# Causal attention feeding two feed-forward layers on one core: where the transposes of the probabilities stand in the traced order

## The chip, the cores and the metric

One core of one Trainium2 chip. The metric is the device time of one execution in microseconds: 579.84 us is the median of three runs of the kernel before (579.39 to 580.96).

## What is computed

```
attention: q, k, v of shape (2, 12, 448, 64); per head
    scores = q @ k.T / 8;  causal mask;  p = exp(scores - rowmax);  p = p / (sum(p) + 1e-9)
    out = p @ v                                  -> x of shape (896, 768)
layer 1:  h = relu(x @ w_in); y = (h * h) @ w_out          (768 -> 2048 -> 768)
layer 2:  8 experts; each token goes to the expert with the largest cosine logit,
          out = gate * (relu(y @ w1[e]) @ w2[e])           (768 -> 1024 -> 768)
```

The routing must choose the same expert as an fp32 computation, so the kernel computes in split precision: an operand is kept as a rounded high part and a low part (the rest), and a product is three matmuls, high by high, high by low, low by high.

## The kernel before

**Tiling of the attention.** A unit is one batch and one pair of heads, so there are 12 units. The 448 queries of a head are cut into seven blocks of 64, and one matmul works on the same block of both heads (2 x 64 = 128 rows). Block c needs (c + 1) x 64 keys.

**What is done for a unit.**
- `s_load` (line 162) loads q and k in one DMA and v in another. `s_prep` (line 174) splits them: ScalarE (ACT) writes the high part of q into the tile `qs`, VectorE (DVE) the low part, and two DMAs on SyncE's queue (SP) copy `qs` into `q2` (line 196), where the two heads stand in separate halves. There are two buffers of `qs` and two of `q2`. GpSimd (POOL) makes the low part of k, and the low part of v in `s_prep_v` (line 199).
- `s_scores` (line 210) takes a block: three matmuls into one bank of PSUM (tile `s`, four banks, line 221), then a masked maximum on DVE (line 231), then the exponential on ACT (line 233), which writes `p` to SBUF and frees the bank.
- `s_norm` (line 236) divides: a reciprocal on DVE (line 241), and for each block a multiplication on POOL (line 245). It comes in two groups, the blocks 2, 0, 1, 3 and the blocks 6, 4, 5.
- `s_trans` (line 255) takes one of the four entries of `BANKS` (line 250): four transposes of 128 x 128 on TensorE (PE) fill one bank of PSUM (tile `pt`, three banks in turn), ACT copies the bank to SBUF as the high part (600 ns or so) and DVE subtracts that from the bank as the low part, which frees the bank. Batch 0 needs the blocks 0 to 3, batch 1 the blocks 4 to 6, batches 2 and 3 blocks of both groups.
- `s_pv` (line 268) multiplies by v in four parts j = 0 to 3 (24 matmuls in all). Part 0 reads the transposes of batches 0 and 1, parts 1 and 2 those of batches 2 and 3, part 3 those of batch 1, with 64 rows instead of 128. `s_x` (line 286) then takes the result out of PSUM with ACT and DVE.

**The order.** The loop near the end of the attention walks through half-steps. For every half-step a string says in which order the pieces are traced: `p` is `s_prep`, `s0` to `s2` are up to three groups of score blocks, `n` is `s_norm`, `t0` to `t3` are the four batches of `s_trans`, `v0` to `v3` the four parts of `s_pv`, `w` is `s_prep_v`. In the even half-step of unit u the scores are the blocks 6 (`s0`) and 4, 5 (`s1`) of unit u + 1, the norm is that of the blocks 2, 0, 1, 3 of unit u + 1, the transposes are of unit u and the parts of `s_pv` of unit u - 1. In the odd half-step the scores are the blocks 2, 0, 1 (`s0`) and 3 (`s1`) of unit u + 2 and the norm that of the blocks 6, 4, 5 of unit u + 1.

The traced order is a priority and not yet the order of execution. A planner walks through a simulated timeline, and on each engine takes the earliest traced instruction whose inputs and buffers the timeline has ready; matmuls of a later piece can so stand between two transposes of one batch. The result is a fixed order for each engine, and on the chip each engine runs its own in that order, waiting on semaphores.

**After the attention.** The matmuls of layer 1 (`phase_a`, lines 303 to 305) are traced behind it, and the planner puts the first of them between the transposes and `s_pv` matmuls of the last two units.

```
        for x in CFG["seq"][h].split():
            i = int(x[1])
            ...
            if x[0] == "t" and 0 <= u < NU:
                s_trans(units[u], i)
            if x[0] == "v" and u >= 1:
                s_pv(units[u - 1], i)
```

Of the kernel before, what the change touches and what calls it, by code (L numbers as in the profile page):

```python
# [32 lines left out]
def f32(ap):  # L33
# [6 lines left out]
    turn2=[1, 3], ft0=[0, 1, 2, 3, 4], ft1=[3], ft2=[2, 4, 5, 6], ew=[2, 4, 10, 10, 10, 12, 14], stop=0, mlo="V", xh="A", h2="A",  # L40
    wh="G", wil="G", wol="GV", warm=6, nsa=6, nwi=3, nwb=3, wo0=4, hs0=[4, 5, 8, 9], conv0=17, convs=2, pin=1,
    qsb=2, pb=2, ptb=2, qkraw=3, vraw=2, vb=2, ss=4, pts=3, pvs=1, pas=4, wsp=1, mz="G",
    seq=("p0 s0 n0 t0 v0 s1 v1 s2 t1", "n0 t2 s0 v2 v3 t3 s1 s2 w0"),
    ch=(((2, 0, 1), (3,), ()), ((6,), (4, 5), ())), wn=[1], qh="A", qdir=1, qss=2, rpin=5, qdma="SS", kh="V",
    vh="AG", kl="G", vl="G", pth="AAAA", nrm="GGGGGGG", u0=1, order=[2, 1, 3, 0, 4], pm=1)

# [1148 lines left out]
```

## Time and profile before

| | |
|---|---|
| median of 3 runs | 579.84 us |
| the profiled execution | 578.43 us, of it 576.7 us between the first and the last instruction |
| PE busy | 552.8 us (96%), 3424 matmuls |
| DVE busy | 397.5 us (69%) |
| ACT busy | 290.8 us (50%) |
| POOL busy | 197.1 us (34%) |
| chain of waits that ended last | 82% on PE |
| attention scores on PE (line 221, high part of k) | 168 matmuls, mean 347 ns from issue to end |
| transposes on PE (line 262) | 192, mean 278 ns from issue to end |
| copies of transposes on ACT | 48, mean 600 ns |
| subtractions of transposes on DVE | 48, mean 682 ns |

A matmul's own duration overlaps with the next one's, so the time that it costs is read from the distance between starts, or from the chain of waits, which counts each stretch once.

### The profile page before, as it was taken

To read this page: it belongs to the slowest core of one execution; us is meant where nothing else is said; L and a number is where in the kernel's file an instruction comes from. 1 tells how busy PE (TensorE), PEld (TensorE's weight loads), DVE (VectorE), ACT (ScalarE), POOL (GpSimd) and SP (SyncE) were. 2 spreads that over 40 slices of the span, in tenths; PEclk is the share of its full clock that TensorE was granted. 3 is DMA by queue.
4 is the path that set the end of the run, shared out by engine and by line. 5 is a ranking of instruction groups with operands and counts; after the bars stand their busy time and mean duration, and the time that the engine had idled before them with its cause. 6 is when DMAs were issued, how large, how long until landed. Compare 5 with 4: busy or idle time off the path is not lost.

```text
span 576.7 us, 9694 instructions
## 1 busy us (share of the span) xinstructions
PE 552.8 (96%) x3424; PEld 509.6 (88%) x3424; DVE 397.5 (69%) x956; ACT 290.8 (50%) x654; POOL 197.1 (34%) x228
## 2 busy tenths in 40 slices
PE   7999999999999999999999999899998999999994
PEld 4999899989999999999899999799997887799993
DVE  7888878855687967796663466973487976932641
ACT  4878777424425243415233217611468877914651
POOL 7677788936535543311000001002204701500010
PEclk8799999999999999999999999999999999899998
DMA  7658433332536445351000019205777987940310
GB/s 230 174 144 269 102 86 77 116 110 98 165 116 212 164 165 178 128 190 55 1 29 27 28 45 409 95 2 197 283 260 251 341 301 258 342 155 29 111 51 5
DMA packets 28234, 86.52 MB, mean 150 GB/s; under 512 B 2822, under 2 KB 13062, under 8 KB 28176
## 3 DMA queue, kind: packets, MB, share of 16 engines
q1 hardware_dynamic: 26640, 79.51, 42.4%
q0 software_dynamic: 1536, 6.29, 3.0%
q8 instruction: 29, 0.48, 0.3%
q14 instruction: 29, 0.24, 0.1%
HBM read 75.24 MB, written 6.29 MB: 141 GB/s over the span
## 4 chain that ended last, share of the span: by engine, by line
PE 82%; DVE 6%; ACT 4%; DMA 3%; issue 2%; SPq 0%; POOL 0%; POOLq 0%; ACTq 0%; DVEq 0%
PE yps L515 19%; PE ops L812 8%; PE pa L303 7%; PE pa L305 7%; PE pa L304 7%; PE pv L279 7%; PE s L221 5%; DVE ml L66 3%; PE pt L262 3%; PE hps L722 3%; PE hps L738 2%; PE hps L737 2%; PE hps L739 2%; PE ops L754 2%; PE ops L749 2%
## 5 line engine op out<-in xcount | busy, mean ns | idle before, releaser
L66 DVE TENSOR_TENSOR ml<-xraw,mh 128x768 fp32r<-128x768 f32 x64 | 60.1, 954 | 15.0 <-ACT mh L59 14.9
L59 ACT ACTIVATE mh<-xraw 128x768 fp32r<-128x768 f32 x64 | 53.3, 845 | 18.3 <-PE ops L749 8.5
L221 PE MATMUL s<-kh,q 128*128 128x128 f32 (+6 forms) x168 | 52.0, 347 | 3.0 <-ACT p L233 2.6
L812 PE MATMUL ops<-mh,act 128*128 128x384 f32 x224 | 53.5, 341 | 0.0
L834 POOL DMA_INDIRECT out<-osb,fsi x10 | 23.6, 2358 | 86.3 <-ACT osb L829 63.9
L279 PE MATMUL pv<-pt,v 128*128 128x448 f32 (+7 forms) x288 | 49.9, 304 | 0.0
L245 POOL TENSOR_SCALAR p<-p,rs 128x192 f32<-128x192 f32 (+6 forms) x84 | 42.5, 525 | 11.2 <-DVE rs L241 10.8
L846 POOL DMA_INDIRECT xr<-ydram,fgi x10 | 14.9, 1490 | 88.3 <-DVE fsi L624 47.0
L123 DVE SCALAR_TENSOR_TENSOR w<-raw,w 128x768 int32<-128x768 int32 x32 | 43.1, 1350 | 0.7
L279 PEld LDWEIGHTS pv<-pt,v 128*128 128x128 f32 (+3 forms) x288 | 37.6, 162 | 5.9 <-DVE pt L66 0.3
L233 ACT ACTIVATE p<-s,mn 128x192 f32<-128x192 f32 (+6 forms) x84 | 39.5, 477 | 6.0 <-DVE mn L231 2.6
L66 DVE TENSOR_TENSOR ml<-mraw,mh 128x768 fp32r<-128x768 f32 x32 | 30.1, 953 | 14.4 <-ACT mh L59 14.4
L812 PEld LDWEIGHTS ops<-mh,act 128*128 128x128 f32 x224 | 39.3, 188 | 0.8
L221 PEld LDWEIGHTS s<-kh,q 128*128 128x128 f32 x168 | 34.4, 214 | 6.2 <-ACT p L233 4.7
L66 DVE TENSOR_TENSOR hs<-h,hs 128x512 fp32r<-128x512 f32 (+1 forms) x32 | 21.9, 691 | 23.9 <-ACT hs L59 23.7
L119 DVE TENSOR_SCALAR w<-raw 128x768 int32<-128x768 int32 x32 | 24.2, 755 | 20.3 <-POOL wi3l L66 7.3
L66 DVE TENSOR_TENSOR pt<-pt 128x512 fp32r<-128x512 f32 x48 | 32.5, 682 | 6.9 <-ACT pt L59 6.3
L121 DVE SCALAR_TENSOR_TENSOR w<-raw,w 128x768 int32<-128x768 int32 x32 | 34.5, 1080 | 0.7
L309 ACT ACTIVATE relu<-pa 128x448 f32<-128x448 f32 x32 | 17.1, 538 | 35.3 <-PE pa L305 35.1
L231 DVE CUSTOM_DVE_ANT_0 s<-s,maskf 128x192 f32<-128x192 f32 (+6 forms) x77 | 31.8, 430 | 3.7 <-PE s L221 3.2
L59 ACT ACTIVATE pt<-pt 128x512 fp32r<-128x512 f32 x48 | 28.0, 600 | 10.5 <-PE pt L262 10.3
L262 PE MATMUL pt<-ident,p 128*128 128x128 f32 x192 | 31.7, 278 | 0.0
(462 smaller groups left out, 1646.3 us busy)
## 6 DMA issues: line engine op xcount, KB each, us to landing
xraw<-in_wm SPq DMA_DIRECT2D x32, 768.0 KB, 5.7
raw<-in_w_in SPq DMA_DIRECT2D x16, 768.0 KB, 4.2
raw<-in_w_out SPq DMA_DIRECT2D x16, 768.0 KB, 4.2
mraw<-in_wm SPq DMA_DIRECT2D x16, 768.0 KB, 5.9
qk<-in_qkd SPq DMA_DIRECT2D x11, 448.0 KB, 4.3
q<-qs SPq DMA_DIRECT2D x22, 224.0 KB, 3.8
v<-in_vd SPq DMA_DIRECT2D x12, 256.0 KB, 3.8
ydram<-ysb SPq DMA_DIRECT2D x7, 384.0 KB, 2.3
```

Source lines behind the costliest of these rows:

```text
L59: A.activation(out, in_, AF.Copy, scale=scale)
L66: eng.tensor_tensor(out=lo, in0=x, in1=hi, op=ALU.subtract)
L123: V.scalar_tensor_tensor(out=w[:, x], in0=raw[:, x, 0], scalar=29, in1=w[:, x], op0=ALU.logical_shift_right, op1=ALU.bitwise_or)
L221: T.matmul(ss, d["q2"][:, c, :, :, x].rearrange("p a b -> p (a b)"), d[y][:, :n], start=i == 0, stop=i == 2 and not first)
L245: G.tensor_scalar(out=p, in0=p, scalar1=rs[:, COL[c]:COL[c] + 1], scalar2=1.0, op0=ALU.mult, op1=ALU.mult)
L262: T.transpose(pt[:, o * P:(o + 1) * P], d["p"][c][:, j * P:(j + 1) * P], ident)
L279: T.matmul(d["pv"][:, j * P:S] if h else d["pv"][0:D, j * P:S], d[x][0:k, j, 1:3].rearrange("p a b -> p (a b)") if h else d[x][0:k, j, 0], ...
L303: T.matmul(ps, wh[:, c], xhi[:, kc, gs], start=(kc == 0), stop=False)
L304: T.matmul(ps, wh[:, c], xlo[:, kc, gs], start=False, stop=False)
L305: T.matmul(ps, wl[:, c], xhi[:, kc, gs], start=False, stop=(kc == KC - 1))
L515: T.matmul(ps[t][c][:, :384], x, w[:, c * 384:(c + 1) * 384], start=(f == 0 and w is wh and x is hi), stop=(f == NF - 1 and x is lo))
L812: T.matmul(ps[c], x, ww[:, c * 384:(c + 1) * 384], start=(fc == 0 and x is hh and ww is wh), stop=(fc == 7 and x is hl))
```

## The change

The two strings of the order are replaced. In the even half-step batch 1 moves from the last place to the one behind batch 0; in the odd half-step batch 3 moves from behind `v3` to the place behind batch 2. Nothing else differs: the same instructions, tiles, buffers and engines.

```diff
-    seq=("p0 s0 n0 t0 v0 s1 v1 s2 t1", "n0 t2 s0 v2 v3 t3 s1 s2 w0"),
+    seq=("p0 s0 n0 t0 t1 v0 s1 v1 s2", "n0 t2 t3 s0 v2 v3 s1 s2 w0"),
```

## Rows read from the trace of the kernel before

**Rows 1.** The page's first part: busy time, share of the span, instructions
```profile
PE 552.8 (96%) x3424; PEld 509.6 (88%) x3424; DVE 397.5 (69%) x956; ACT 290.8 (50%) x654; POOL 197.1 (34%) x228
```

**Rows 2.** Stretches of time, with each engine's busy time in it
```profile
core 0: us, PE busy (x) PEld busy (x) DVE busy (x) ACT busy (x) POOL busy (x), PEclk, DMA share, GB/s
16.00:20.40 4.40, 4.40 (x19) 4.23 (x20) 3.18 (x14) 2.82 (x12) 2.88 (x5) 0.51 0.98 246
30.00:104.00 74.00, 73.36 (x529) 66.65 (x529) 61.31 (x201) 57.97 (x177) 58.83 (x104) 1.00 0.52 139
104.00:126.00 22.00, 22.00 (x140) 19.42 (x139) 16.02 (x28) 7.17 (x16) 14.86 (x15) 1.00 0.26 77
126.00:230.00 104.00, 104.00 (x515) 96.21 (x514) 77.21 (x70) 39.29 (x70) 48.72 (x30) 1.00 0.49 160
```

**Rows 3.** Who waited for whom, 20 to 104 us: total us, times, longest
```profile
PE s L221 <- ACT p L233: 0.5, 1, 0.5
...
PEld s L221 <- ACT p L233: 2.4, 7, 0.7
...
ACT qs L59 <- DMA q<-qs: 8.7, 6, 2.3
```

**Rows 4.** The chain of waits, 62 to 84 us: start, us, what
```profile
68.57 0.81 PE s L221 x3
...
73.06 0.33 PE s L221 x3
...
80.72 0.44 PE pt L262 x4
...
82.26 0.51 PE s L221 x3
...
83.33 0.59 PE pt L262 x4
```

**Rows 5.** PE in order of time, 118 to 122 us: start, us, instructions
```profile
118.75 1.03 PE L262 MATMUL pt<-ident,p 128*128 128x128 f32 x8
...
119.83 0.60 PE L262 MATMUL pt<-ident,p 128*128 128x128 f32 x4
```

**Rows 6.** All engines in order of time, 62 to 70 us
```profile
61.95 0.68 DVE L66 TENSOR_TENSOR pt<-pt 128x512 fp32r<-128x512 f32 x1
...
62.82 0.60 PE L262 MATMUL pt<-ident,p 128*128 128x128 f32 x4
...
65.24 0.61 ACT L59 ACTIVATE qs<-qk 128x448 fp32r<-128x448 f32 x1 [2.29 <-DMA q<-qs]
65.26 0.66 PE L262 MATMUL pt<-ident,p 128*128 128x128 f32 x4
...
68.06 0.37 ACT L233 ACTIVATE p<-s,mn 128x128 f32<-128x128 f32 x1
...
68.40 0.60 ACT L59 ACTIVATE pt<-pt 128x512 fp32r<-128x512 f32 x1
...
68.57 0.45 PE L221 MATMUL s<-kh,q 128*128 128x384 f32 x1 [0.47 <-ACT p L233]
```

**Rows 7.** All engines in order of time, 82 to 91 us
```profile
84.04 1.70 POOL L245 TENSOR_SCALAR p<-p,rs 128x448 f32<-128x448 f32 x3 [0.31 <-DVE rs L241]
...
86.16 0.27 PE L262 MATMUL pt<-ident,p 128*128 128x128 f32 x1
86.19 1.76 PE L279 MATMUL pv<-pt,v 128*128 128x448 f32 x8
...
88.11 0.49 PE L262 MATMUL pt<-ident,p 128*128 128x128 f32 x3
```

**Rows 8.** All engines in order of time, 16 to 24 us
```profile
17.73 0.63 PE L262 MATMUL pt<-ident,p 128*128 128x128 f32 x2
...
18.33 1.70 POOL L245 TENSOR_SCALAR p<-p,rs 128x448 f32<-128x448 f32 x3 [1.16 <-DVE rs L241]
...
21.14 0.60 PE L262 MATMUL pt<-ident,p 128*128 128x128 f32 x4
```

## The prediction

> **What bounds the kernel now.** I read the busy times first, then stretches, waits, and the chain. The busy times show PE at 96% of the span and the next engine, DVE, at 69% [rows 1]. Cut into stretches, the attention's steady part from 30 to 104 us has PE busy for 73.36 of 74.00 us at full clock, and DVE, ACT and POOL for 61.31, 57.97 and 58.83 us [rows 2]. So PE sets the pace there, with the three others at 78 to 83%, close enough that a queue in the wrong order can hold PE up. From 104 to 230 us PE is busy in every microsecond [rows 2], with the matmuls of layer 1 filling all that the last two units leave. What is won or lost on PE before 104 us is therefore passed on whole to the end.
>
> The waits show how much there is to win. Between 20 and 104 us PE stood still once, for 0.5 us, and its weight loads seven times for 2.4 us, all for the same thing: the exponential of a score block that had not yet freed its PSUM bank [rows 3]. The reason is one line further down: ACT stood 8.7 us in six waits, the longest 2.3 us, with a high part of q at the head of its queue, until the DMA that still read the `qs` buffer was done; the exponentials queue behind it [rows 3]. One such place is seen in order of time: ACT waits 2.29 us and starts on `qs` at 65.24, the exponential of block 1 comes at 68.06, and at 68.57 PE, idle for 0.47 us, starts block 5 [rows 6].
>
> **The change part by part.**
>
> *The transposes themselves.* Their number stays at 192 in 48 batches. On the chain a batch of four costs 0.44 us, 0.11 us each [rows 4]. The trace already has eight in a row, near the end: their row lasts 1.03 us where the row of four lasts 0.60 [rows 5], so the second four add 0.43, again 0.11 each. Batches of eight are no cheaper and no dearer: 0.00 us, with 0.01 per pair of batches, 24 x 0.01 = 0.24 us, as the bound on the good side and nothing on the bad.
>
> By the Trainium skill ("TensorE: Matmul & The Clock Gate", Part 4: PE-mode transpose) transposes do not count as PE being busy for the clock gate, which speaks against packing them. Here the stretch that holds the eight and the four has its clock granted in full, 1.00 [rows 2], against the rule for a pack of this size. What the rule would cost is the last rival below.
>
> *Behind `v3`.* Batch 3 now runs behind the 64-row matmuls of `v3`, and costs 0.59 us on the chain instead of 0.44 [rows 4]. In the new order a score block stands there. A score block behind 64-row matmuls costs 0.51 us where the same block elsewhere costs 0.33 [rows 4]. The 0.15 that the transposes save the scores pay with 0.18. I take 0; the bounds are -0.15 x 9 = -1.4 us (nine of the twelve units lie in the steady part) and +0.03 x 9 = +0.3.
>
> *Batch 1 ahead of `v0` and of the blocks 4 and 5.* It cannot move far: it needs the blocks 4 to 6 normed. In the unit that I followed POOL norms them from 84.04 to 85.74, the batch's first transpose is at 86.16 and the other three at 88.11, behind eight matmuls with v [rows 7]. So the three can move up by at most about 2 us, into the matmuls with v, and the PE work is merely permuted. Where they get in front of block 5, this block ends 0.44 us later, and what hangs on it is the DMA that refills `q2` (it waits for block 5 of two units before), then ACT's wait for the `qs` buffer, then the exponentials. Behind the waiting `qs` on ACT stand exponentials and copies, behind these DVE's subtractions, and PE waits for all of them. Bounds: 0, where PE has other work, as in all but one of the places of rows 3; 0.44 x 6 = 2.6 us, if each of the six waits of ACT is carried through. I take it once, at the one place where PE itself already stands idle: +0.44 us.
>
> *Batch 3 ahead of the blocks 2, 0, 1 and of `v2`, `v3`.* It moves up from 65.26 to about 63.26, right behind batch 2 (62.82 + 0.44) [rows 6]. It needs the PSUM bank of batch 0, three banks back, whose subtraction ends at 61.95 + 0.68 = 62.63 [rows 6]: free, with 0.63 us to spare. Its copy on ACT, now at 68.40 behind the exponential of block 1 [rows 6], can then stand ahead of the exponentials of 2, 0 and 1, and these each end one copy, 0.60 us, later. But the three exponentials wait in the same queue behind `qs` either way. If the copy goes ahead of `qs`, it is done in ACT's idle time and the backlog behind is 0.60 us shorter; if behind, 0.60 us longer. Bounds -0.60 and +0.60 at each of the six places, -3.6 and +3.6 us, cut on the good side to the 2.4 us of weight-load waits that exist. I take 0, since nothing in the rows says which of the two the planner picks. The DVE subtraction moves with the copy. No DMA is issued by a step that moves; SP's and POOL's queues hold the same instructions, and in the odd half-step the norm still stands first.
>
> *The start.* Up to the first transposes nothing changes. The clock is at half there (0.51 from 16.00 to 20.40 [rows 2]). Batch 1 of the first unit can't come before POOL is done with its blocks at 18.33 + 1.70 = 20.03, and it stands at 21.14 [rows 8]: at most 1.1 us, in a part of PE's queue that is full anyway. 0 us.
>
> *The end of the attention.* In the last two units the transposes stand between matmuls of layer 1 and PE has no gap at all [rows 2]: 0 us.
>
> **Sum.** 0 + 0 + 0.44 + 0 + 0 + 0 = +0.4 us on a span of 576.7. The profiled execution took 578.43 us with what lies around the span, so 578.8; the median of three runs lies 1.4 above the profiled one, so 580.2 us. A difference under 0.3% of the time, 1.7 us, can't be told from none.
>
> **The rivals.**
>
> *A, slower: ACT's waits grow.* The place is the `qs` at the head of ACT's queue. Batch 1 ahead of block 5 delays the refill of `q2` by 0.44 us per unit, the copy of batch 3 falls behind `qs`, and in the six units with an ACT wait PE waits 0.44 us more: 6 x 0.44 = 2.6, 582.4 us. With the copy's 0.60 on top at three of the six, 4.4 us, 584.2. For it: DVE and ACT have little slack, and the wait chain already reaches PE. Against: in six of seven cases PE had enough queued that it lost under half a microsecond. It decides from 1.7 us on, four of six places carried through.
>
> *B, slower: the PSUM banks.* Batch 3 right behind batch 2 finds the bank of batch 0 still being read. The spare time is 0.63 us at the place that I followed [rows 6]. If DVE is later by more than this and PE then waits 0.25 us in each of nine units, 2.3 us: 582.1. Against: a subtraction that the planner sees as late lets it put other matmuls first.
>
> *C, faster: the waits go.* Batch 3's copy runs in ACT's idle time, the 2.4 us of weight-load waits shrink to a fifth or so, and the 0.15 us behind `v3` is saved in three units: 1.9 + 0.45 = 2.4, 577.4 us. For it: the idle time of 2.29 us is there and the copy needs 0.60. Against: the planner must put it ahead of `qs` by its own timeline, in which this DMA need not be late.
>
> *D, nothing moves.* The norms on POOL end just before batch 1 starts, and the planner lets other matmuls pass whatever waits. Then PE's order is nearly the same and the time is 579.8, within the forecast's bound.
>
> *E, the clock.* Were the half clock of the start to last to the end of the fourth batch at 23.7 us because more transposes stand there, the 3.3 us from 20.4 on would yield half their work: +1.6 us, 581.4. The page named above would have it so; the full clock beside the eight transposes speaks against it, and so does the fact that batch 1 hardly moves there.
>
> **How the numbers follow.** Forecast 0.35, A 0.25, B 0.08, C 0.20, D 0.10, E 0.02. Forecast and D together give 0.45 for no difference; A, B and E 0.35 for slower; C 0.20 for faster. The likeliest stands at 580.2. The range reaches down to C's 577.4 with 0.2 of spread, 577.2, and up to A's upper case, 584.2: below and above lie about one in ten each, mostly A carried through in more units.
>
> **What would show it.** In the changed kernel's trace: rows of eight transposes of about 1.03 us between 30 and 104 us, or fours parted by other matmuls, if D holds. PE busy within 0.5 us of 73.4 in a 74 us stretch; scores behind `v3` at about 0.51 us. The waits of `s` for `p` tell A from C: above 4 us for A, under 1 us for C. B shows as transposes that wait for DVE's subtraction, which the trace of before does not have. E shows in the granted clock from 20 to 24 us. The prediction is wrong if the attention ends more than 1.7 us earlier or later, or if the stretches behind 126 us, which I take as shifted and otherwise the same, change their length.

## The result and the profile after

The changed kernel took 584.22 us in the median of its runs (580.20 to 588.14), the kernel before 580.72 in the runs beside them (577.37 to 583.38). The ratio is 1.0064, with a 95% interval of [1.0047, 1.0081]: slower by 0.64%, which is 3.7 us (the two medians are 3.5 apart), and more than the 0.3% that can be told from no change. The forecast of 580.2 was wrong, and the median stands just beyond the upper end of the range, 584.2. The profiled execution took 583.35 us with a span of 581.5 us, 4.8 us more than before.

Busy times of the changed kernel, answering to [rows 1]: PE's share stays at 96%, and this view tells nothing.

```profile
PE 556.2 (96%) x3424; PEld 511.7 (88%) x3424; DVE 396.8 (68%) x956; ACT 290.3 (50%) x654; POOL 197.3 (34%) x228
```

The stretches of [rows 2] in the changed kernel, with 20.4 to 24 and 60 to 90 us added; the columns are those of [rows 2].

```profile
16.00:20.40 4.40, 4.40 (x21) 4.19 (x21) 3.63 (x13) 2.51 (x11) 2.59 (x5) 0.60 0.91 244
20.40:24.00 3.60, 3.55 (x26) 2.96 (x26) 3.41 (x17) 3.60 (x15) 2.40 (x5) 1.00 0.76 146
30.00:104.00 74.00, 71.00 (x487) 63.12 (x488) 55.31 (x183) 51.24 (x162) 51.61 (x93) 0.98 0.48 126
60.00:90.00 30.00, 27.49 (x178) 23.85 (x177) 19.61 (x68) 19.11 (x60) 19.45 (x36) 0.94 0.37 89
104.00:126.00 22.00, 21.90 (x143) 19.63 (x142) 15.90 (x32) 10.29 (x27) 21.05 (x25) 1.00 0.35 109
126.00:230.00 104.00, 104.00 (x521) 95.83 (x520) 79.27 (x77) 38.07 (x69) 48.47 (x30) 1.00 0.46 149
```

The kernel before from 60 to 90 us:

```profile
60.00:90.00 30.00, 29.48 (x213) 26.57 (x211) 23.78 (x82) 23.40 (x73) 22.87 (x40) 1.00 0.45 104
```

PE lost 2.36 us of busy time in the steady part (73.36 to 71.00), 1.99 of them from 60 to 90 us, where it ran 178 matmuls in place of 213. The three other engines did less there too, 3.4 to 4.3 us each: nobody became the bound, they all stood still. Busy time understates the loss, since part of it ran at half clock, as the last section tells: from 30 to 104 us PE ran 487 matmuls in place of 529, and at the pace of before (74.00 us for 529) the 42 that are missing are worth 5.9 us, an estimate. The loss reaches layer 1 whole. Its last weight tile, before and after (x12: shortest, median, longest in ns, first and last start in us), comes 5.6 us later:

```profile
L303 PE MATMUL pa<-xhi,wi15h x12: 362/365/369, 226.3 to 233.0; 128*128 128x448 f32 x12
```

```profile
L303 PE MATMUL pa<-xhi,wi15h x12: 362/365/369, 231.9 to 238.6; 128*128 128x448 f32 x12
```

At the end of the profiled execution 4.8 us of it are left, and 3.5 between the medians; where the rest is made up is not shown.

The waits of the changed kernel, 20 to 104 us, answering to [rows 3] (total us, times, longest):

```profile
ACT qs L59 <- DMA q<-qs: 12.4, 7, 3.9
...
PEld s L221 <- ACT p L233: 4.9, 10, 1.0
ACT p L233 <- PE pt L262: 3.8, 2, 2.0
...
PE s L221 <- ACT p L233: 2.1, 5, 0.8
...
PE pt L262 <- DVE pt L66: 0.4, 1, 0.4
```

ACT's wait in front of `qs` grew from 8.7 to 12.4 us, its longest from 2.3 to 3.9, and PE's waits for the exponentials from 0.5 and 2.4 to 2.1 and 4.9. The place of the longest one, all engines in order of time (start, us, instructions, in brackets the idle time before), answers to [rows 6]:

```profile
61.40 3.22 PE L279 MATMUL pv<-pt,v 128*128 128x448 f32 x20
...
62.34 0.60 ACT L233 ACTIVATE p<-s,mn 128x384 f32<-128x384 f32 x1
...
64.55 1.53 PE L262 MATMUL pt<-ident,p 128*128 128x128 f32 x12
...
66.94 0.62 ACT L59 ACTIVATE qs<-qk 128x448 fp32r<-128x448 f32 x1 [3.92 <-DMA q<-qs]
...
67.44 0.41 ACT L233 ACTIVATE p<-s,mn 128x192 f32<-128x192 f32 x1
...
67.83 1.57 ACT L59 ACTIVATE pt<-pt 128x512 fp32r<-128x512 f32 x3
...
68.00 0.48 PE L221 MATMUL s<-kh,q 128*128 128x448 f32 x1 [0.25 <-ACT p L233]
...
69.30 0.63 PE L262 MATMUL pt<-ident,p 128*128 128x128 f32 x4 [0.42 <-DVE pt L66]
...
70.21 0.35 ACT L233 ACTIVATE p<-s,mn 128x64 f32<-128x64 f32 x1
...
70.71 0.64 PE L221 MATMUL s<-kh,q 128*128 128x320 f32 x1 [0.78 <-ACT p L233]
```

Twenty matmuls with v and then twelve transposes run in a row while ACT waits for the DMA. At 66.94 ACT is let go with `qs`, an exponential and three copies of transposes in its queue, and the exponential of block 0 comes at 70.21. PE has nothing left to do meanwhile but wait for the banks, at 68.00, 69.30 and 70.71. ACT's wait of 3.92 us is 1.6 longer than the 2.29 of before [rows 6], and ACT comes to it at the same time, 63.0 us. The DMA that ends it was issued 0.4 us later (at 61.21 against 60.79) and took 1.2 us longer until ACT was released (5.7 us against 4.5); why it took longer is not shown.

The chain of waits shows what follows one unit later (start, us, what). In before's chain [rows 4] no DMA stands between 62 and 84 us; here one does.

```profile
72.73 0.97 PE s L221 x3
...
75.07 4.25 DMA q<-qs
...
79.48 0.61 ACT qs L59
```

The unit's last score block is late, the two DMAs that refill its `q2` are issued only behind it (the second one at 75.07), and the next `qs` waits for them until 79.48. Behind v3 [rows 4] and in the places of [rows 7, 8] nothing adds up to this: rows of eight hardly occur between 30 and 104 us (fours and twelves do), and near the end, where before had a row of eight [rows 5], there are twelve:

```profile
124.34 1.47 PE L262 MATMUL pt<-ident,p 128*128 128x128 f32 x12
```

PE's order in the program shows why. Each letter is a run of matmuls: s scores, t transposes, v matmuls with v. Two units of the steady part, first before, then after:

```
t4 s6 t3 s3 t1 s3 t1 v8 s3 t3 v4 t4 s3 v1 s3 v11 t4 s6 t4 s6 t4 v8 s3 v4 t4 v2 s3 v3 s3 v7
t4 s3 t4 s3 t4 s3 v16 s3 v2 t4 s3 v6 s6 t3 s3 t1 s6 v21 t12 s6 v3 s6
```

With batch 3 early, a unit's matmuls with v are all ready early. By `BANKS` it reads the blocks 4 to 6 alone, and not blocks of both groups, so it waits for no norm that batch 1 has not waited for. Batch 1 of the next unit still waits for its norms on POOL, so the planner lets some twenty of them pass it, and batches 1, 2 and 3 then come out together, in three units of the steady part.

### The profile page after: what moved, and what is told of

Read it like the earlier page. It is cut to its first block, busy times and chain, and to the rows that moved or that the text cites. A ratio compares the mean times of both kernels' runs of the same rounds, so it can differ in the third digit from the quotient of the medians.

```text
span 581.5 us, 9698 instructions
## 1 busy us (share of the span) xinstructions
PE 556.2 (96%) x3424; PEld 511.7 (88%) x3424; DVE 396.8 (68%) x956; ACT 290.3 (50%) x654; POOL 197.3 (34%) x228
## 4 chain that ended last, share of the span: by engine, by line
PE 78%; DVE 8%; ACT 4%; issue 3%; POOL 3%; DMA 2%; SPq 1%; POOLq 0%; ACTq 0%; DVEq 0%
PE yps L515 19%; PE ops L812 10%; PE pa L305 7%; PE pa L303 7%; PE pa L304 7%; PE pv L279 4%; DVE ml L66 4%; PE s L221 4%; PE hps L722 3%; PE pt L262 2%; PE hps L738 2%; PE hps L737 2%; PE hps L739 2%; POOL p L245 2%; PE ops L754 2%
## 5 line engine op out<-in xcount | busy, mean ns | idle before, releaser
L221 PE MATMUL s<-kh,q 128*128 128x128 f32 (+6 forms) x168 | 53.5, 357 | 3.9 <-ACT p L233 3.7
L279 PE MATMUL pv<-pt,v 128*128 128x448 f32 (+7 forms) x288 | 46.1, 300 | 0.0
```

The lines of the kernel that those rows point to most:

```text
L221: T.matmul(ss, d["q2"][:, c, :, :, x].rearrange("p a b -> p (a b)"), d[y][:, :n], start=i == 0, stop=i == 2 and not first)
L279: T.matmul(d["pv"][:, j * P:S] if h else d["pv"][0:D, j * P:S], d[x][0:k, j, 1:3].rearrange("p a b -> p (a b)") if h else d[x][0:k, j, 0], ...
```

## The experiments

**Theory A**: the loss is ACT's wait in front of `qs`; the new order makes it reach PE and feeds it back through `q2`. **Theory B**: it is the lumpy order itself, which starves ACT and DVE and then floods them. Ratios are against the kernel before, run beside each.

**Which half of the change.** e8 moves batch 3 alone, e7 moves it half the way:

```diff
-    seq=("p0 s0 n0 t0 v0 s1 v1 s2 t1", "n0 t2 s0 v2 v3 t3 s1 s2 w0"),
+    seq=("p0 s0 n0 t0 v0 s1 v1 s2 t1", "n0 t2 t3 s0 v2 v3 s1 s2 w0"),   # e8
+    seq=("p0 s0 n0 t0 v0 s1 v1 s2 t1", "n0 t2 s0 t3 v2 v3 s1 s2 w0"),   # e7
```

> Only the odd half-step's string replaced, the even one as before. The planner gives each engine the same instructions in the same order as in the changed kernel, so every theory expects its time: slower than the kernel before by 0.4 to 0.9%, 582.5 to 586 us. It shows whether the loss is there again beside the other kernels of this call.

> The kernel before with batch 3 moved only half of the way, behind the scores of the blocks 2, 0, 1 and still ahead of the matmuls with v. The planner then puts batches 0 and 1 in a row of eight ahead of 15 to 18 matmuls with v, and has no row of twelve before 104 us. Theory B: no lump of 20 and 12, so within 1.7 us of the kernel before. Theory A: ACT's waits for the DMA decide; above 11 us the time is 583 us or more, under 9 us it is that of the kernel before. If long runs of matmuls with v alone cost (16 to 18 are here too), 582 us or more.

e8: 584.95 us, 1.0078 [1.0050, 1.0106]. Its instructions stand in the changed kernel's order on every engine; with the even string alone replaced, they stand in the order of before on every engine, so that half needed no run. The whole effect is batch 3's. Its profile has no half clock between 30 and 104 us, and layer 1's last tile comes 4.3 us later than before, against 5.6 in the changed kernel; the 1.3 us between them fit the half clock told of at the end.

```profile
L303 PE MATMUL pa<-xhi,wi15h x12: 362/365/369, 230.7 to 237.3; 128*128 128x448 f32 x12
```

e7: 581.77 us, 1.0029 [1.0004, 1.0053], a loss at the edge of what can be told from none. There eight transposes stand in a row in the steady part, twelve never. ACT waits 6.7 us for `qs`, less than in the kernel before, and yet PE's waits for the exponentials, 2.4 and 4.5 us, are those of the changed kernel: neither sum alone sets the loss.

**Eight in a row.** e4 puts both batches of a pair last. Batches 2 and 3 then read blocks of p that a later unit has partly overwritten, so that part of the computation is changed; the work is the same.

```diff
+    seq=("p0 s0 n0 v0 s1 v1 s2 t0 t1", "n0 s0 v2 v3 t2 t3 s1 s2 w0"),
```

> The changed kernel with both pairs of batches moved to the end of their half-step's matmuls with v (batches 0 and 1 last in the even half-step, 2 and 3 behind v3 in the odd one), so that eight transposes do stand in a row but behind the scores. Theory A: the scores of block 5 come earlier, so do the refill of q and ACT's split; ACT's waits for the DMA under 8.7 us, 577 to 581 us. Theory B: rows of eight transposes give ACT and DVE two copies in a lump but no run of 20 matmuls ahead of them; 579 to 583 us. If eight in a row is what costs, whatever stands ahead of it: 583 us or more.

581.31 us, 1.0009 [0.9986, 1.0033], with rows of eight in each unit of the steady part, at 1.03 to 1.09 us, the price of [rows 5]:

```profile
49.85 1.03 PE L262 MATMUL pt<-ident,p 128*128 128x128 f32 x8
...
58.05 1.03 PE L262 MATMUL pt<-ident,p 128*128 128x128 f32 x8
```

Rows of eight cost nothing here; what costs is where batch 3 stands.

**Room for qs, planned anew.** e1 is the changed kernel, e2 the one before, with four of the eleven `qs` tiles (units 2, 3, 6, 7) in buffers that lie free during the attention:

```diff
+    qraw=[2, 3, 6, 7]
-            q = apool.tile([P, NQ, QC, 2], F32R, tag="qs", bufs=CFG["qss"], name="qs")
+            if units.index(u) in CFG["qraw"]:
+                q = spool.tile([P, NQ, QC, 2], F32R, tag="raw", name="qs")
+            else:
+                q = apool.tile([P, NQ, QC, 2], F32R, tag="qs", bufs=CFG["qss"], name="qs")
```

> The changed kernel with two more buffers for the split q (units 2, 3, 6 and 7 take a staging buffer that is idle then), so that ACT seldom finds the buffer still read by a DMA. Theory A (the exponentials queue on ACT behind the split of q, which waits for that DMA; 12.4 us of such waits in the changed kernel against 8.7 before): the waits fall under 4 us between 20 and 104 us, PE's weight loads wait for exponentials under 2.5 us, and the time comes back to the kernel before or below, 577 to 582 us. Theory B (the planner's new order is itself lumpy: some 20 matmuls with v in one run, then 12 transposes, so that ACT and DVE first starve and then have three copies ahead of the exponentials): ACT's waits for the DMA fall as well, but the lumps and most of the loss stay, 582.5 to 586 us.

> The kernel before with the same two extra buffers, as the control. Theory A: ACT's waits for the DMA (8.7 us) fall under 3 us and PE's 2.4 us of waits for exponentials under 1 us; the time falls by 1 to 2 us against the kernel before. Theory B: no lumps here, so nothing to win but the same 1 to 2 us at most. If the extra buffers alone cost or win more than 3 us, the first kernel of this call is to be read against this one and not against the kernel before.

e1: 580.96 us, 0.9998 [0.9979, 1.0017]; the loss is gone. e2: 580.96, 0.9990 [0.9971, 1.0010], without the 1 to 2 us that were expected of it. In e1 the steady part is full, PE busy for 73.88 of 74.00 us. Layer 1's last tile still starts 2.5 us later than before in its profile (228.9 us), and that was lost at the start: from 20.4 to 24.0 us PE is busy for 1.03 us where before has 3.59. This fits A, but the planner had made a new order for e1 too, in which twenty matmuls with v and twelve transposes never stand in a row in the steady part, so B is not excluded.

**Batch 1 not passed over.** In e3 the changed kernel's first matmuls with v may not be planned ahead of batch 1's last transpose, an order without a wait:

```diff
+                    if i == CFG["hold"] and u < NU:
+                        es.enter_context(tc.issue_after(last["t", 1].ins))
                     s_pv(units[u - 1], i)
```

> The changed kernel with the matmuls of the first part with v held on PE's queue until the second batch of transposes of the same step has been issued, so that the two batches of the even half-step can't be pushed behind the matmuls with v. Theory B: the runs of 12 transposes behind 20 matmuls with v go (one run of 20 is left, at the end), and with them most of the loss: 578 to 582.5 us, the granted clock between 60 and 90 us full. Theory A: the refill of q's buffers still hangs on the scores of block 5, which stand as late as in the changed kernel; ACT's waits for the DMA stay above 10 us and the time above 582.5 us. A third outcome, PE waiting more than 3 us for the norms on POOL at the held place, would show why the planner passes the second batch over.

581.27 us, 1.0002 [0.9978, 1.0026]. The lump of twenty and twelve is gone, ACT's wait is 6.5 us (longest 1.8), and so is the loss, as B expected; A had expected waits above 10 us. Either the room (e1) or the order (e3) undoes it, and neither run holds the other fixed.

**The order held fixed.** From here on each instruction of PE, DVE, ACT and POOL, and SP's apart from the loads of the raw weights, is tied behind the one that preceded it on its engine in another kernel, by an order alone and no wait:

```diff
-    in_attn = False
+    in_attn = replay(tc)     # abridged: for a, b in zip(names, names[1:]): add_manual_dep(b, a, NoSync)
```

e5 has the room of e1 in the changed kernel's order. e6 has the two buffers in e1's order.

> The first kernel of the series (changed strings, two more buffers for the split q) with the changed kernel's own order of instructions pinned for the attention on PE, ACT, DVE and POOL, and on SP but for the weight loads: 20 matmuls with v and 12 transposes in a row are back, only the buffers differ from the changed kernel. Theory A (the wait for the buffer of the split q is the loss): ACT's waits for that DMA under 4 us between 20 and 104 us and the time at the kernel before, 578 to 582 us. Theory B (the lumpy order is the loss, whatever the buffers): 583 us or more, with PE's weight loads waiting over 4 us for exponentials. If both are needed together, 580 to 583.

> The changed kernel, with its two buffers for the split q, and the order of instructions of the first kernel of the series pinned for the attention. Theory A: without the extra buffers ACT stands behind the DMA again, 8 us or more between 20 and 104 us, and the time goes up to 583 us or more. Theory B: the order has no run of 20 matmuls before 12 transposes between 30 and 104 us; 579 to 582.5 us, whatever ACT waits.

e5: 583.95 us, 1.0065 [1.0035, 1.0094]. It looks like B, but its rows, ACT's wait and the stretches, say otherwise:

```profile
ACT qs L73 <- DMA q<-qs: 7.2, 2, 4.3
```

```profile
30.00:60.00 30.00, 30.00 (x219) 27.60 (x218) 24.93 (x83) 24.22 (x74) 24.26 (x44) 1.00 0.66 174
60.00:90.00 30.00, 27.44 (x192) 23.94 (x190) 20.64 (x72) 20.10 (x63) 20.58 (x37) 1.00 0.43 111
```

The five waits up to unit 9 were gone, and there PE is full. The two that stayed, 4.3 and 2.9 us, are those of units 10 and 11, which reuse the buffers of 8 and 9, and PE's loss stands there too. The experiment had left the two costliest waits in place and could not decide.

e6: 613.36 us, 1.0565 [1.0530, 1.0600], far outside what either theory said. An order made for the larger room issues `qs` too early for two buffers:

```profile
ACT qs L73 <- DMA q<-qs: 29.7, 6, 8.3
...
PE s L235 <- ACT p L247: 16.6, 7, 4.1
```

It does not tell A from B about the change, but it shows at full size what a blocked head of ACT's queue does to PE. Part of the 33 us is the clock, which is 0.81 on average from 30 to 104 us there.

**The order held, and no wait left.** e9 is e5 with unit 10's tile moved too, so that unit 11 follows unit 8 in its buffer. e10 has the same room in the order of before. PE, DVE, ACT and POOL stand in exactly the order of the changed kernel and of the one before; only loads of raw weights come later.

```diff
-    qraw=[2, 3, 6, 7]
+    qraw=[2, 3, 6, 7, 10]
```

> The changed kernel's own order, the same on PE, DVE, ACT and POOL, with more room for the split q: the qs tiles of the units 2, 3, 6, 7 and 10 lie in buffers that stand free during the attention (those of the raw weights), so that no qs needs a buffer that was in use less than three units before, units 10 and 11 included; the loads of two raw weights come later for it. Theory A (the loss comes from ACT standing at the head of its queue before qs, until the DMA that reads its buffer is done): the ACT waits for that DMA fall from 12.4 us to under 1.5, PE is busy for at least 29.3 of the 30 us from 60 to 90 (changed kernel 27.49, before 29.48), and the time is within 0.25% of the kernel before, 579.5 to 582 us. Theory B (the order itself, twenty matmuls with v and then twelve transposes in a row, which starves and then floods ACT and DVE): the waits go all the same, PE stays at 27.4 to 28.2 us in that stretch, and the time stays at 583 to 585 us.

> The kernel before in its own order on PE, DVE, ACT and POOL, with the same room for the split q as the run beside it (units 2, 3, 6, 7 and 10 in the buffers of the raw weights). Theory A: the ACT waits for the DMA of qs fall from 8.7 us to under 1.5; PE stood for only some 0.5 us of idle and 2.4 us of weight-load waits because of them, so the time falls by 0.5 to 2 us against the kernel before, ratio 0.996 to 0.999. Theory B, in which qs does not matter: the waits go and the time stays within 0.1% of before. Both expect this run to be the floor for the one beside it; its distance to that run is what the order alone costs once qs waits for nothing.

e9: 578.51 us, 0.9960 [0.9939, 0.9981]. e10: 577.94 us, 0.9955 [0.9931, 0.9978]. No ACT wait for the DMA of `qs` is left in either. PE in e9, then in e10:

```profile
30.00:104.00 74.00, 73.93 (x534) 67.65 (x534) 63.03 (x202) 58.66 (x180) 59.15 (x102) 1.00 0.51 136
...
60.00:90.00 30.00, 30.00 (x223) 27.73 (x222) 24.06 (x80) 23.18 (x73) 22.94 (x43) 1.00 0.62 166
```

```profile
30.00:104.00 74.00, 74.00 (x544) 68.10 (x542) 61.92 (x204) 60.33 (x182) 61.69 (x104) 1.00 0.53 140
```

The place shown of the changed kernel, in e9: `qs` starts at 60.60 without a wait, the twelve transposes follow the matmuls with v all the same, and the scores follow them without a gap.

```profile
59.20 3.17 PE L279 MATMUL pv<-pt,v 128*128 128x448 f32 x20
...
60.60 0.64 ACT L59 ACTIVATE qs<-qk 128x448 fp32r<-128x448 f32 x1
...
62.30 1.53 PE L262 MATMUL pt<-ident,p 128*128 128x128 f32 x12
...
63.32 1.56 ACT L59 ACTIVATE pt<-pt 128x512 fp32r<-128x512 f32 x3
...
63.58 0.28 PE L221 MATMUL s<-kh,q 128*128 128x64 f32 x1
```

The next row of twelve transposes, the same instructions in the same order in the changed kernel, e5 and e9:

```profile
86.31 1.53 PE L262 MATMUL pt<-ident,p 128*128 128x128 f32 x12
```

```profile
84.33 1.53 PE L279 MATMUL pt<-ident,p 128*128 128x128 f32 x12
```

```profile
79.09 1.53 PE L262 MATMUL pt<-ident,p 128*128 128x128 f32 x12
```

The row before it starts at 64.55, 63.45 and 62.30: e5 is 1.2 us behind e9 there and 5.2 behind one row later, and between the two lie its two waits.

So A holds. In the very same lumpy order the loss turns into a gain when the wait goes, and with no wait the two orders are 0.6 us apart, well within both intervals. The lumpy order costs only together with the two buffers: A is the cause, and the order is what lets it through to PE. The loads of raw weights that come later hardly explain it: from 60 to 90 us, where the loss was, the DMA engines are busier in e9 than in the changed kernel, 0.62 against 0.37. e9 came out faster than A expected (579.5 to 582 us). e10 and e9 both beat both kernels; e10 is the fastest run here, 0.45% below before. It gains about what was expected, a ratio of 0.996 at best. The gain stands where the last waits were: eight matmuls with v start at 60.33 us, as in the kernel before (60.30), and the twelve transposes behind the steady part at 105.53 against 106.87. At layer 1's last tile, e9 and e10 are ahead of before by 1.1 and 1.3 us:

```profile
L303 PE MATMUL pa<-xhi,wi15h x12: 362/365/369, 225.2 to 231.9; 128*128 128x448 f32 x12
```

```profile
L303 PE MATMUL pa<-xhi,wi15h x12: 362/365/369, 225.0 to 231.7; 128*128 128x448 f32 x12
```

That is less than the 1.6 and 2.2 us between the medians; what the rest is stays open, one profile each being too little for half a microsecond.

## Why the prediction was wrong, step by step

- *The transposes themselves*: right. e4 has its eights at 1.03 to 1.09 us and a time that can't be told from before. The kernel before had even a row of twelve, at 106.87 us, which the prediction passed over.
- *Behind `v3`*: the exchange of scores and transposes at this place hardly took place as pictured, since the order changed as a whole; no row bears on the 0.
- *Batch 1 ahead of `v0` and of the blocks 4 and 5*: costed at +0.44, and it is 0, because the planner gives the same order with and without this half. That is rival D for this half. The text had the reason (the norms on POOL end only just before) and should have drawn that conclusion.
- *Batch 3 ahead of the blocks 2, 0, 1 and of `v2`, `v3`*: **this step failed.** It stood at 0, with bounds of -2.4 and +3.6, and it is the whole result: +3.5 us by the medians, and +4.6 in e8, which moves batch 3 alone. It was worked out as one copy of 0.60 us that falls ahead of or behind a waiting `qs`. What it did was to make the matmuls with v ready earlier, so that they ran ahead of batch 1 and used up, while ACT was waiting, the work that before had covered PE; e3, in which they may not pass batch 1, has no loss. That the bound of +3.6 was near is luck, since it came from the copy. The prediction asked what the batch overtakes; it had to ask also what the batch releases.
- *The start* and *the end of the attention*: as predicted, no loss is seen there. Layer 1 from 126 us on is shifted and otherwise the same, its last tile taking 6.7 us in both. That a delay is passed on whole to the end, as the prediction has it, is borne out up to this tile and not beyond: of 5.6 us there 4.8 are left at the end.
- *Rival A* named the place (`qs` at the head of ACT's queue), its sign (waits of `s` above 4 us; they are 2.1 and 4.9) and, in its upper case, the size (584.2). Its path was in part another: it went by batch 1 in front of block 5 and the place of a copy, and what held ACT and PE up were a DMA that took longer, the missing cover and, one unit later, the refill of `q2` behind late scores. That its sum met the measured time is therefore luck.
- *Rival B*, the banks: one wait of 0.4 us, and that behind ACT's block. *Rival C* had the gain that lies in the waits about right (2.4 us; e10 is 2.2 us below before) but not the edit that brings it.
- *Rival E*, the clock: from 16.0 to 20.4 us the clock is 0.60 and not lower, from 20.4 to 24.0 it is 1.00, and it does not fall beside the twelve transposes at 64.55. The Trainium skill says that a transpose doesn't count as a busy PE in the same way ("TensorE: Matmul & The Clock Gate", Part 4: PE-mode transpose). No effect of this is seen in e9, which holds its clock at 1.00 from 60 to 90 us with the same twelve. A half clock did come later in the changed kernel, as the last section tells.

## What to carry to other kernels

When a step is moved in a program whose order a planner makes, ask what the step releases as well as what it overtakes: the work that it makes ready may be the cover of a wait elsewhere. An engine that stands at the head of its queue for a DMA is a debt even while the others hide it, so cost an edit near it by what is left to run when it stands, and consider paying it off first: more buffers there gained 0.45% on the order of before, and made both orders equal within the noise. An experiment that takes a wait away has to be read for the waits that it left, before its time is believed.

## What the runs showed of the hardware

The granted clock fell to half in the changed kernel just after PE's waits at 68.00 to 70.71. PE in order of time, in the changed kernel and then in e8, at the same instructions: a matmul of the scores takes 0.47 us in place of 0.31, and four transposes 1.06 in place of 0.60.

```profile
71.14 0.47 PE L221 MATMUL s<-kl,q 128*128 128x320 f32 x1
...
71.67 1.06 PE L262 MATMUL pt<-ident,p 128*128 128x128 f32 x4
```

```profile
70.85 0.31 PE L221 MATMUL s<-kl,q 128*128 128x320 f32 x1
...
71.15 0.60 PE L262 MATMUL pt<-ident,p 128*128 128x128 f32 x4
```

In the stretch from 60 to 90 us the granted clock is 0.94 on average for it. e8, with the same instructions in the same order and nearly the same waits, kept 1.00 there, so the fall is not certain to come; what decides it was not settled. It also falls elsewhere in some executions, as from 364 to 371 us in e10 where before kept 1.00, and spans of single profiles differ by that:

```profile
364.00:371.00 7.00, 5.73 (x26) 5.08 (x26) 6.89 (x15) 3.02 (x6) 0.00 (x0) 0.76 0.00 1
```

A DMA that copies half of `qs` took 3.4 us from issue to landing at the least in the kernel before, from 60 to 80 us; in the changed kernel the wait at 66.94 ended 5.7 us after the second one's issue at 61.21, and in e5 5.3, against 4.5 in the kernel before. What slows them there stays open.
